# A LayerNorm's transposes: eight row tiles turned by DMA in f16 halves in place of TensorE f32 transposes

## The chip, the cores and the metric

One core of a Trainium2 chip runs the whole program. The time is that of one execution on the device in microseconds; the kernel before was run three times, 1746.54 to 1746.77 us, with a median of 1746.63. A change of time is counted against that median.

## The reference

A transformer block with adaptive LayerNorm over 2048 rows of 512: attention over the last 512 cached keys (32 query heads, 8 key heads), then a GEGLU feed-forward, each behind a LayerNorm whose scale and shift come from a conditioning vector `c`.

```
mod = (silu(c) @ w_mod).reshape(c.shape[0], 6, 1, -1)
sa, ca, ga, sb, cb, gb = (mod[:, 0], ..., mod[:, 5])
h = layernorm(x) * (1 + ca) + sa
x = x + ga * attention(h)          # q = h @ wq, softmax(q k^T / sqrt(128)) v, @ wo
h = layernorm(x) * (1 + cb) + sb   # the second LayerNorm
x = x + gb * ((gelu(h @ w_gate) * (h @ w_up)) @ w_down)
```

All is f32. The kernel keeps f32 exactness on the f16 matrix engine by splitting each operand into two f16 halves, a high one and the remainder, and adding three products of halves.

## The kernel before, in words

The 2048 rows are 16 tiles of 128. Attention runs in two halves of the rows, 0 to 1023 and 1024 to 2047. A loop over steps `t` goes through 512 score tiles (128 queries by 512 keys, one head); 256 belong to the first half of the rows, 256 to the second. In a step TensorE computes one score tile `ps` as three f16 matmuls into one of two PSUM banks, VectorE takes the negated row maximum `nm` (line 974), ScalarE the exponential `ee` (983), two steps later ScalarE scales it into the high f16 half of `p` (995), and three steps later VectorE makes the low half (1000) and SP's queue turns both halves with one DMA transpose, `pt<-p` (1004). Up to three groups of other matmuls follow in each step, popped from a list: the q projection (Strassen products, banks `qa`, `qb`, `qc`), P times V (`po`, which reads `pt` two units of four steps later), and the output projection (`py`). PSUM banks under the tag "acc" are five, handed round in turn; p's f16 tiles are four.

Every engine runs its instructions in the order in which the program gives them while this loop lasts. Work beside the main stream is placed by step: `at(("w", t), fn)` puts `fn`'s instructions behind everything else of step `t`, `("d", t)` behind the low half of p on VectorE. Transfers go through SP's queue in program order; `spare` fills steps that moved nothing with a transfer from a list of due ones.

When the last of the output projections of a row tile is added to `acc` (line 943), `attn_final` is called. For the first eight tiles, which are finished as the second half of the attention begins, it starts the second LayerNorm at once: `ln_tile(2, ti, ...)` returns the steps `stat` (row mean and variance on VectorE, 378 to 382, and the power -0.5 on GpSimd, 388), `norm` (subtract and multiply in place on `acc` on GpSimd, through `pool_ts`, 236), `turn` (four f32 transposes by TensorE into one "acc" bank `pln`, 491), `affine` twice (two ScalarE pieces of 128 columns each from `pln` into `hf` with scale and shift, 499; the second also stores `hf` to DRAM as `hs`), and `parts` twice (f16 high halves on ScalarE, 511, low halves on GpSimd, 513). They are placed 1, 5, 8, 9, 10, 12 and 13 steps after the call. Twelve steps after it the next rows of x are loaded into the tile's `acc` buffer. GpSimd also prepares weights in this time: it scales them (159), makes high halves (155), subtracts for the low halves (156) and forms the Strassen sums (789).

The last eight tiles' second LayerNorm (`ln_turned`, in the feed-forward) is turned by DMA already. The stored `hs` are read again by the `combos` for the feed-forward, from step 478 on. The feed-forward itself follows the loop.

Of the kernel before, what the change touches and what calls it, by code (L numbers as in the profile page):

```python
# [11 lines left out]
F16 = mybir.dt.float16  # L12
BF16 = mybir.dt.bfloat16
AF = mybir.ActivationFunctionType
ALU = mybir.AluOpType
AX = mybir.AxisListType

P = 128
S, D, F = 2048, 512, 1792
HQ, HKV, DH = 32, 8, 128  # L20
W = 512
KT = D // P
# [39 lines left out]
def block_kernel(ctx: ExitStack, tc: tile.TileContext, x, kT, v, wq, wo, wg, wu, wd, cT, wc, wm, out):  # L62
    nc = tc.nc

    const = ctx.enter_context(tc.tile_pool(name="const", bufs=1))
    pool = ctx.enter_context(tc.tile_pool(name="pool", bufs=2))
# [4 lines left out]
    def tmp(name):  # L71
        return pool.tile([P, 512], F32, tag="e", name=name, bufs=NE)

    def raw(name):
        return pool.tile([P, 512], F32, tag="raw", name=name, bufs=NRAW)
# [4 lines left out]
    def bank(tag, name, bufs):  # L80
        return psum.tile([P, 512], F32, tag=tag, name=name, bufs=bufs)
# [9 lines left out]
    def dma(out_, in_):  # L91
        moved[0] += 1
        nc.sync.dma_start(out_, in_)

    def load_acc(i, src, eng=None):
        acc[i] = pool.tile([P, D], F32, tag="acc", name="acc", bufs=2 * QT)
        (eng.dma_start if eng else dma)(acc[i], src)

    def rows_of(t, i):
        return t[i * P:(i + 1) * P, :]  # L100
# [134 lines left out]
    def pool_ts(out, src, a, b=1.0, op0=ALU.mult, op1=ALU.mult):  # L235
        nc.gpsimd.tensor_scalar(out, src, a, b, op0=op0, op1=op1)
# [111 lines left out]
    def spilled(gen, key):  # L348
        if (gen, key) not in hs:
            n = KT if key in (0, 1) else 2  # L350
            hs[gen, key] = dram.tile([P, n, QB], F32, name=f"hs{gen}_{key}")
        return hs[gen, key]

    def block(gen, name):
        if (gen, name) not in BK:
            BK[gen, name] = pool.tile([P, 4, QB], F16, tag="h", name=name, bufs=NB)
        return BK[gen, name]
# [15 lines left out]
    def ln_cols(key):  # L373
        return (1, 0) if key == "a" else (4, 3)

    def ln_stat(a, st, act=False):
        bn = small.tile([P, 6], F32, name="bn")
        nc.vector.bn_stats(bn, a)
        st["mv"] = small.tile([P, 2], F32, name="mv")
        nc.vector.bn_aggr(st["mv"], bn)  # L380
        st["rs"] = small.tile([P, 1], F32, name="rs")
        nc.vector.tensor_scalar(st["rs"], st["mv"][:, 1:2], EPS, None, op0=ALU.add)
        if act:
            st["nm"] = small.tile([P, 1], F32, name="nmean")
            nc.vector.tensor_scalar(st["nm"], st["mv"][:, 0:1], -1.0, None, op0=ALU.mult)

    def ln_power(st):
        nc.gpsimd.tensor_tensor(st["rs"], st["rs"], nhalf, op=ALU.pow)
# [69 lines left out]
    def ln_last(i):  # L458

        st = {}  # L460
        ln_stat(acc[2 * QT + i], st)
        ln_power(st)
        rs, nm = col("kmax", i), col("kinv", i)
        pool_ts(rs, st["rs"], 1.0)
        pool_ts(nm, st["mv"][:, 0:1], st["rs"], -1.0)

    def ln_tile(gen, i, src):
        jsc, jsh = ln_cols("a" if gen < 2 else "f")
        qb, i = divmod(i % (2 * QT), QT)
        st = {}  # L470

        def load():
            if gen == 2:
                st["x"] = src()
            else:
                st["x"] = raw("xs")
                dma(st["x"], src())

        def stat():
            ln_stat(st["x"], st)  # L480
            ln_power(st)

        def norm():
            if gen == 2:
                return pool_ts(st["x"], st["x"], st["mv"][:, 0:1], st["rs"], ALU.subtract, ALU.mult)
            nc.vector.tensor_scalar(st["x"], st["x"], st["mv"][:, 0:1], st["rs"], op0=ALU.subtract, op1=ALU.mult)

        def turn():
            st["ps"] = bank("acc", "pln", NACC)
            for dt in range(KT):  # L490
                nc.tensor.transpose(st["ps"][:, dt * P:(dt + 1) * P], st["x"][:, dt * P:(dt + 1) * P], ident)

        def affine(dts):
            if 0 in dts:
                st["f"] = raw("hf") if gen == 2 else tmp("hf")
            f = st["f"]
            for dt in dts:
                sl = slice(dt * P, (dt + 1) * P)
                nc.scalar.activation(f[:, sl], st["ps"][:, sl], AF.Identity,
                                     scale=cols[:, jsc, dt:dt + 1], bias=cols[:, jsh, dt:dt + 1])  # L500
            if KT - 1 in dts:
                dma(spilled(gen, qb)[:, :, i * P:(i + 1) * P], f.rearrange("p (k q) -> p k q", k=KT))

        def parts(act):
            o = slice(i * P, (i + 1) * P)
            f = st["f"].rearrange("p (k q) -> p k q", k=KT)
            for h, name in enumerate(("b11", "b21") if qb == 0 else (None, "b22")):
                if name:
                    t, src = block(gen, name), f[:, 2 * h:2 * h + 2, :]
                    if act:  # L510
                        nc.scalar.activation(t[:, 0:2, o], src, AF.Copy)
                    else:
                        nc.gpsimd.tensor_tensor(t[:, 2:4, o], src, t[:, 0:2, o], op=ALU.subtract)

        more = [lambda: parts(True), lambda: parts(False)]
        return load, [stat, norm, turn, lambda: affine((0, 1)), lambda: affine((2, 3))] + more

    TURN = {}

# [149 lines left out]
    def k_items(pr):  # L669
        g = pr // 2  # L670
        st, load = reader(kT[g])
        m = {}

        def stat():
            m["m"] = little("lm", 4, dtype=BF16)
            sumsq(m["m"][:, 0:1], st["r"])

        def spread(go=True, ps=None):
            return k_spread(g, m["m"], go, ps)

        def parts(first=False):
            KV[0, pr, 0] = t = get_k()
            if first:
                return split_post(t, st["r"], col("ksc", pr))
            times(st["r"], col("ksc", pr))
            halves(t, st["r"])

        return (load, stat, spread, parts) + ((m,) if pr == 0 else ())
# [33 lines left out]
    def at(key, *fns):  # L722
        later.setdefault(key, []).extend(fns)
# [95 lines left out]
    def plain_steps(key, by):  # L819
        def part(k):  # L820
            SET.setdefault(key, [None, None])[k] = get_w(k)
            if key > 1:
                return soon(split_post(SET[key][k], RAW[key][k], by))
            times(RAW[key][k], by)
            halves(SET[key][k], RAW[key][k])

        return lambda: part(0), lambda: part(1)
# [121 lines left out]
    def attn_final(ti):  # L949
        y1[ti] = dram.tile([P, D], F32, name=f"y{ti}")  # L950
        dma(y1[ti], acc[ti])
        nxt = (ti + 2 * QT) % NT
        if ti < 2 * QT:
            own, steps = ln_tile(2, ti, lambda: acc[ti])
            own()
            for d, fn in zip((1, 5, 8, 9, 10, 12, 13), steps):
                at(("w", now[0] + d), fn)
            at(now[0] + 12, lambda: load_acc(nxt, rows_of(x, nxt)))
        else:
            ln_last(ti - 2 * QT)  # L960
            at(now[0] + 3, lambda: load_acc(nxt, y1[nxt]))
# [31 lines left out]
    def high(t):  # L993
        p16 = pool.tile([P, 2, W], F16, tag="p16", name="p16", bufs=NP16)
        nc.scalar.activation(p16[:, 0, :], E[t]["e"], AF.Copy, scale=E[t]["r"])  # L995
        E[t]["p16"] = p16

    def low(t):
        p16 = E[t]["p16"]
        nc.vector.scalar_tensor_tensor(p16[:, 1, :], E[t]["e"], E[t]["r"], p16[:, 0, :], op0=ALU.mult, op1=ALU.subtract)  # L1000
        u, i = divmod(t, 4)
        if i == 0:
            pT[u] = pool.tile([P, QT, 2 * KT, P], F16, tag="pt", name="pt", bufs=NPT)
        nc.sync.dma_start_transpose(pT[u][:, i], p16.rearrange("p a b -> p (a b)"))
        E.pop(t)
# [196 lines left out]
    for g in range(NG):  # L1202
# [6 lines left out]
        if 0 < g < GW:  # L1209
            a, b = plain_steps(g, by)  # L1210
            sched_pair(g, srcs, t0 - (19 if g > 1 else 13), spread, [(t0 - (13 if g > 1 else 8), a)], [(t0 - (11 if g > 1 else 7), b)])
        elif g >= GW and (not half or pr < GW):
            sched_set(g, srcs, t0, by, spread)
            if not half:
                a, b, c, d, e, f = SETPOS2 if g == GW else SETPOS
# [11 lines left out]
        else:  # L1227
            if g > 0:
                if pr % 2 == 0:
                    load, stat, spread_, parts = k_items(pr)  # L1230
                    sched(t0 - (22 if g > 2 else 20), (load, [stat]))
                    at(("w", t0 - (19 if g > 2 else 17)), spread_)
                load, stat, spread_, parts = k_items(pr)
                sched(t0 - (7 if g > 2 else 8 if g > 1 else 6), (load, [parts if g != 2 else lambda parts=parts: soon(parts(True))]))
                at(t0 - (3 if g > 2 else 1 if g > 1 else 2), lambda pr=pr: store(("k", pr), KV[0, pr, 0]))
                if pr % 2 == 0:
                    load, stat, spread_, parts = v_items(qd)
# [159 lines left out]
    for n in range(NP):  # L1397
        b = T // 2 + 30 + 27 * n
# [167 lines left out]
    for i in range(2 * QT):  # L1566
        q = 7 * (2 + i // 2) + 3 * (i % 2)
        load, norm, split, turn = ln_turned(i)
# [6 lines left out]
    for p in range(2):  # L1575
        q = 51 + 14 * p
# [67 lines left out]
```

## Time and profile before

| | us |
|---|---|
| median of three runs | 1746.63 |
| the profiled execution | 1747.24 |
| its span, first to last instruction | 1745.3 |
| TensorE busy in the span | 1723.9 |
| VectorE busy | 1380.3 |
| ScalarE busy | 1213.7 |
| GpSimd busy | 901.1 |

In the rows of the profile PE is TensorE, PEld its weight loads, DVE VectorE, ACT ScalarE, POOL GpSimd, SPq the instruction queue of SyncE, which issues the DMAs. A timeline row has its start, its duration, engine, line, operation, output and inputs by name, their shapes, and in square brackets how long the engine was idle before it and what ended that. The end of a matmul is modelled and overlaps the next start. Groups that are listed by line give a count and the least, median and largest duration in ns. A line is that of the kernel before; line 87 is the helper that issues all f16 matmuls.

### The profile page before, as it was taken

Reading aid. Unit: us, or ns where it says so; the run is one execution under the profiler, and the core shown is the slowest. Engines: PE = TensorE matmul, PEld = TensorE weight load, DVE = VectorE, ACT = ScalarE, POOL = GpSimd, SP = SyncE. Lnnn points to the kernel's source line nnn. Section 1 sums busy time; section 2 is a strip of 40 time slices with the busy share of each in tenths; the row PEclk is TensorE's granted clock in tenths of the full one; section 3 lists DMA queues with packets and bytes.
Section 4 is the critical chain, followed back from the end, with each engine's and each line's share of the span. In section 5 each row is a group of like instructions: output and inputs, shape, how many; then the busy total and the mean of one; then the engine's idle time right before and its main releaser. Section 6 shows DMA issues by size and latency. Waiting matters only on the chain.

```text
span 1745.3 us, 25819 instructions
## 1 busy us (share of the span) xinstructions
PE 1723.9 (99%) x8080; PEld 793.2 (45%) x8082; DVE 1380.3 (79%) x2404; ACT 1213.7 (70%) x2751; POOL 901.1 (52%) x1120
## 2 busy tenths in 40 slices
PE   7999999999999999999999999999999999999999
PEld 5444444444444444444444444444444444444444
DVE  7898898888889999888888888888886655555555
ACT  6988788888879777888777777877784544323232
POOL 4889778776788884654475565554521224000000
PEclk9999999999999999999999999999999999999999
DMA  7999999999999999999999999999986753252222
GB/s 234 219 206 211 211 215 206 225 209 219 213 219 228 212 205 183 212 208 235 212 201 215 203 220 199 211 214 213 195 184 145 205 174 117 81 183 77 88 75 76
DMA packets 667498, 329.71 MB, mean 189 GB/s; under 512 B 561504, under 2 KB 580192, under 8 KB 667360
## 3 DMA queue, kind: packets, MB, share of 16 engines
q1 hardware_dynamic: 667072, 327.54, 82.0%
q8 instruction: 64, 1.05, 0.3%
q14 instruction: 74, 0.61, 0.1%
q10 hardware_dynamic: 288, 0.52, 0.1%
HBM read 131.73 MB, written 59.90 MB: 110 GB/s over the span
## 4 chain that ended last, share of the span: by engine, by line
PE 87%; DVE 4%; ACT 4%; issue 1%; DMA 1%; POOL 1%; SPq 0%; ACTq 0%; POOLq 0%; DVEq 0%
PE py L87 25%; PE po L87 17%; PE ps L87 16%; PE fa L87 8%; PE qa L87 8%; PE fc L87 4%; PE qc L87 4%; PE qb L87 2%; PE fb L87 2%; ACT ee L983 1%; DVE p L1000 1%; ACT p L995 1%; DVE nm L974 1%; DMA pt<-p 1%; PE pq L87 1%
## 5 line engine op out<-in xcount | busy, mean ns | idle before, releaser
L983 ACT ACTIVATE ee<-ps,nm 128x512 f32<-128x512 f32 x512 | 350.2, 684 | 199.2 <-DVE nm L974 196.5
L1000 DVE SCALAR_TENSOR_TENSOR p<-ee,rr,p 128x512 f16<-128x512 f32 x512 | 460.7, 900 | 5.1 <-ACT p L995 4.7
L974 DVE TENSOR_REDUCE nm<-ps 128x1 f32<-128x512 f32 x512 | 350.3, 684 | 111.5 <-PE ps L87 108.4
L87 PE MATMUL ps<-k,qt 128*128 128x512 f16 x1536 | 414.9, 379 | 5.4 <-ACT ee L983 4.2
L87 PE MATMUL po<-pt,v 128*128 128x512 f16 x1536 | 373.0, 379 | 2.0 <-DMA pt<-p 2.0
L995 ACT ACTIVATE p<-ee,rr 128x512 f16<-128x512 f32 x512 | 364.4, 712 | 13.1 <-DVE rr L991 8.8
L87 PE MATMUL py<-wo,ot 128*128 128x512 f16 x1536 | 371.5, 379 | 0.0
L87 PEld LDWEIGHTS <-w 128*128 128x128 f16 x2184 | 213.5, 98 | 258.1 <-DVE w L1045 0.6
L87 PEld LDWEIGHTS <-v 128*128 128x128 f16 x1536 | 149.9, 98 | 184.3 <-DMA pt<-p 2.5
L87 PEld LDWEIGHTS <-ot 128*128 128x128 f16 x1536 | 150.2, 98 | 181.7 <-DVE ot L731 0.5
L87 PEld LDWEIGHTS <-qt 128*128 128x128 f16 x1536 | 145.9, 98 | 176.7 <-issue 4.3
L87 PE MATMUL py<-wo,at 128*128 128x512 f16 x672 | 160.5, 379 | 0.0
L943 DVE SCALAR_TENSOR_TENSOR acc<-py,dysc,acc 128x512 f32<-128x512 f32 x112 | 81.5, 747 | 51.1 <-PE py L87 51.1
L731 DVE SCALAR_TENSOR_TENSOR ot<-po,ot 128x512 f16<-128x512 f32 x128 | 87.7, 685 | 33.0 <-ACT ot L730 32.2
L87 PEld LDWEIGHTS <-at 128*128 128x128 f16 x672 | 65.7, 98 | 79.3
L983 ACT ACTIVATION_READ_ACCUMULATOR ee<-ps,nm 128x1 f32 x512 | 99.9, 195 | 0.0
L943 DVE SCALAR_TENSOR_TENSOR acc<-py,ysc,acc 128x512 f32<-128x512 f32 x128 | 94.7, 740 | 6.2 <-PE py L87 6.2
L1281 ACT ACTIVATE at<-fg 128x512 f16<-128x512 f32 x56 | 35.2, 628 | 72.2 <-DVE fg L1279 71.9
L87 PE MATMUL qa<-t,w 128*128 128x512 f16 x348 | 84.9, 379 | 0.0
L87 PE MATMUL fa<-t,w 128*128 128x512 f16 x336 | 82.0, 379 | 0.0
L730 ACT ACTIVATE ot<-po 128x512 f16<-128x512 f32 x128 | 73.9, 577 | 5.0 <-PE po L87 5.0
L232 POOL TENSOR_TENSOR lw<-lw,half__86 128x1 f32<-128x1 f32 x37 | 22.1, 598 | 104.6 <-DVE lw L182 104.5
(222 smaller groups left out, 2379.9 us busy)
## 6 DMA issues: line engine op xcount, KB each, us to landing
w<-kept SPq DMA_DIRECT2D x123, 256.0 KB, 3.2
wo<-kept SPq DMA_DIRECT2D x60, 256.0 KB, 3.8
raw<-in_wo SPq DMA_DIRECT2D x56, 256.0 KB, 3.3
kept<-stage SPq DMA_DIRECT2D x56, 256.0 KB, 3.4
kept<-w SPq DMA_DIRECT2D x39, 256.0 KB, 3.4
rw<-in_wq SPq DMA_DIRECT2D x38, 256.0 KB, 3.2
hs<-hf SPq DMA_DIRECT2D x32, 256.0 KB, 2.9
pt<-p SPq DMA_TRANSPOSE x512, 3.5
```

The lines of the kernel that those rows point to most:

```text
L87: nc.tensor.matmul(ps, a, b, start=first and n == 0, stop=last and n == 2, skip_group_check=chain)
L232: nc.gpsimd.tensor_tensor(out, out, half_, op=ALU.pow)
L730: nc.scalar.activation(t[:, 0, :], src, AF.Copy, scale=scale)
L731: return lambda: nc.vector.scalar_tensor_tensor(t[:, 1, :], src, scale, t[:, 0, :], op0=ALU.mult, op1=ALU.subtract)
L943: nc.vector.scalar_tensor_tensor(acc[ti], st["p"], by, acc[ti], op0=ALU.mult, op1=ALU.add)
L974: nc.vector.tensor_reduce(nm, E[t]["ps"], axis=AX.X, op=ALU.max, negate=True)
L983: nc.scalar.activation(e, E[t]["ps"], AF.Exp, bias=E[t]["nm"], scale=1.0, accum_out=sm[:, t % 2:t % 2 + 1])
L995: nc.scalar.activation(p16[:, 0, :], E[t]["e"], AF.Copy, scale=E[t]["r"])
L1000: nc.vector.scalar_tensor_tensor(p16[:, 1, :], E[t]["e"], E[t]["r"], p16[:, 0, :], op0=ALU.mult, op1=ALU.subtract)
L1281: nc.scalar.activation(t[:, 0, :], g, AF.Copy)
```

## The change

In `ln_tile` with `gen == 2` the step `turn` becomes four steps. `high` copies the normed rows to f16 on ScalarE; `low` subtracts that from them on GpSimd; `turn_dma` turns both halves with one DMA transpose on SP's queue into `lnt`; `joined` adds the two turned halves on VectorE into the f32 tile `hf`. `affine` then works in place on `hf` in SBUF instead of reading a PSUM bank. The steps stand 1, 4, 5, 6, 7, 10, 10, 11, 12 and 13 steps after the call. The new tiles `lnh` and `lnt` have two buffers each; the scratch memory for GpSimd's own DMA descriptors is set to 1024.

```diff
+        def high():
+            st["h"] = pool.tile([P, 2, D], F16, tag="lnh", name="lnh", bufs=2)
+            nc.scalar.activation(st["h"][:, 0, :], st["x"], AF.Copy)
+
+        def low():
+            nc.gpsimd.tensor_tensor(st["h"][:, 1, :], st["x"], st["h"][:, 0, :], op=ALU.subtract)
+
+        def turn_dma():
+            st["t"] = pool.tile([P, 2, KT, P], F16, tag="lnt", name="lnt", bufs=2)
+            nc.sync.dma_start_transpose(st["t"].rearrange("p h k q -> p (h k) q"), st["h"].rearrange("p a b -> p (a b)"))
+
+        def joined():
+            st["f"] = raw("hf")
+            f = st["f"].rearrange("p (k q) -> p k q", k=KT)
+            nc.vector.tensor_tensor(f, st["t"][:, 0], st["t"][:, 1], op=ALU.add)
+            st["ps"] = st["f"]
+
         def affine(dts):
-            if 0 in dts:
-                st["f"] = raw("hf") if gen == 2 else tmp("hf")
+            if 0 in dts and gen < 2:
+                st["f"] = tmp("hf")
...
-        return load, [stat, norm, turn, lambda: affine((0, 1)), lambda: affine((2, 3))] + more
+        turns = [high, low, turn_dma, joined] if gen == 2 else [turn]
+        return load, [stat, norm] + turns + [lambda: affine((0, 1)), lambda: affine((2, 3))] + more
...
-            for d, fn in zip((1, 5, 8, 9, 10, 12, 13), steps):
+            for d, fn in zip((1, 4, 5, 6, 7, 10, 10, 11, 12, 13), steps):
...
-    nc = _bacc.Bacc("TRN2", target_bir_lowering=False, num_devices=1)
+    nc = _bacc.Bacc("TRN2", target_bir_lowering=False, num_devices=1, dynamic_dma_scratch_size=1024)
```

## The prediction

> **What bounds the kernel now.** First the page's busy shares, then the busy time by stretch for the two places around the change, then TensorE's own timeline there.
>
> ```profile
> span 1745.3 us, 25819 instructions
> PE 1723.9 (99%) x8080; PEld 793.2 (45%) x8082; DVE 1380.3 (79%) x2404; ACT 1213.7 (70%) x2751; POOL 901.1 (52%) x1120
> ```
>
> ```profile
> 690.00:800.00 110.00, 108.87 (x524) 51.38 (x522) 95.23 (x179) 93.23 (x229) 59.60 (x62) 1.00 0.96 207
> 800.00:840.00 40.00, 40.00 (x189) 18.17 (x188) 33.04 (x59) 32.59 (x77) 24.65 (x34) 1.00 1.07 233
> ...
> 720.00:735.00 15.00, 14.37 (x72) 6.90 (x70) 14.70 (x29) 11.54 (x28) 14.42 (x14) 1.00 1.07 218
> ```
>
> The columns of a stretch are its length, then busy time and count of TensorE, its weight loads, VectorE, ScalarE and GpSimd, then the granted clock, the DMA engines' share and GB/s. TensorE is busy for 99% of the span at a granted clock of 1.00, so time that is taken from its stream or put into it stays to the end. The eight tiles of the change lie between 690 and 800 us. VectorE works 95.23 of those 110 us, ScalarE 93.23, GpSimd 59.60: none is full on the whole, but between 720 and 735 VectorE has 0.30 us left and GpSimd 0.58. Whatever the change adds there pushes back what stands behind it.
>
> **What is removed.** 32 f32 transposes, four per tile (I number the tiles 0 to 7).
>
> ```profile
> 699.56 0.60 PE L491 MATMUL pln<-ident,acc 128*128 128x128 f32 x4
> 700.00 0.81 PE L87 MATMUL ps<-k,qt 128*128 128x512 f16 x3
> 700.64 2.11 PE L87 MATMUL po<-pt,v 128*128 128x512 f16 x9
> ...
> 730.01 0.81 PE L87 MATMUL po<-pt,v 128*128 128x512 f16 x3
> 731.45 0.63 PE L491 MATMUL pln<-ident,acc 128*128 128x128 f32 x4 [0.63 <-POOL w L155]
> 731.91 0.81 PE L87 MATMUL ps<-k,qt 128*128 128x512 f16 x3
> ...
> 773.18 0.81 PE L87 MATMUL po<-pt,v 128*128 128x512 f16 x3
> 774.31 0.63 PE L491 MATMUL pln<-ident,acc 128*128 128x128 f32 x4 [0.32 <-ACT hf L499]
> 774.77 0.81 PE L87 MATMUL ps<-k,qt 128*128 128x512 f16 x3
> ```
>
> Durations of matmuls overlap, so I count from start to start. Three matmuls of 512 columns take 700.64 - 700.00 = 0.64 us. Tile 0 costs 700.00 - 699.56 = 0.44. Tiles 1, 2, 4, 5 and 6 show the same 0.43 to 0.44 and no wait; with tile 0 that is 2.6. Tile 3 also waits: 731.91 - (730.01 + 0.64) = 1.26. Tile 7: 774.77 - (773.18 + 0.64) = 0.95. Sum 4.8 us.
>
> ```profile
> 730.85 0.46 ACT L499 ACTIVATE hf<-pln,cols 128x128 f32<-128x128 f32 x1
> ```
>
> I put the wait at 731.45 down to this row: it ends at 731.31 and is the last to read tile 2's PSUM bank, and the five "acc" banks are handed round, so tile 3's transposes get that one; GpSimd's norm, the other thing that they need, was long done. Without transposes these eight banks are not asked for, and both waits go. If they only move to the next user of a bank, 4.8 becomes 2.6 + 0.46 + 0.46 = 3.5.
>
> **What is added, per tile.** A ScalarE copy to f16, a GpSimd subtraction, one DMA transpose of 128x1024 on SP's queue, a VectorE addition. The affine steps read SBUF in place of PSUM. The rows, by source line, are counts and least, median and largest ns: a ScalarE copy and a VectorE sum of the same size first,
>
> ```profile
> L1281 ACT ACTIVATE at<-fg x56: 612/630/632, 1335.8 to 1734.5; 128x512 f16<-128x512 f32 x56
> L440 DVE TENSOR_TENSOR b<-hf,b x3: 676/676/677, 20.6 to 40.4; 128x512 f16<-128x512 f32 x3
> ```
>
> then GpSimd's subtraction in two stretches, and the transposes of p from 720 to 750.
>
> ```profile
> L156 POOL TENSOR_TENSOR w<-rw,w x3: 1157/1157/1161, 603.0 to 618.0; 128x512 f16<-128x512 f32 x3
> L156 POOL TENSOR_TENSOR w<-rw,w x2: 1600/1632/1663, 731.5 to 737.4; 128x512 f16<-128x512 f32 x2
> ```
>
> ```profile
> L1004 SPq DMA_TRANSPOSE pt<-p x11: 1231/1232/1348, 721.7 to 749.5; - x11
> DMA to landing us min/median/max: 3.0/3.5/4.9
> ```
>
> ScalarE: 8 x 0.63 = 5.0 us of the 16.8 it has free. VectorE: 8 x 0.68 = 5.4 of 14.8 free; the row has the operation and the size with two SBUF inputs, only the types differ, and I allow 0.5 to 1.2 each. GpSimd: 1.16 to 1.66 each, 9.3 to 13.3 of 50 free; I take 1.16, the middle of the first stretch, since the block of GpSimd's work below already holds stretched rows. The affine from SBUF: the pair of L511 at 736.33, quoted below, reads twice the width from SBUF in 0.71, L499's pair at 716.82 takes 0.83, so I take no change, and 0.2 a pair either way. SP: 1.23 of issue and 3.5 to landing, like the eleven of p in these 30 us. The DMA engines carry it: eight more of 256 KB over 110 us raise 207 GB/s by 19 to 226, and the stretch from 800 to 840 ran 233 GB/s with TensorE busy 40.00 of 40. By busy time alone all of this is hidden and 4.8 stands. The store of a tile's turned rows comes one step later and trades places on SP with a few fetches; the same transfers go out, and the stored rows are read only from step 478 on. The smaller pool that is set aside for GpSimd's own DMA descriptors costs nothing, as no data transfer here is issued by GpSimd; its bound is the 1.94 us that lie around the span, either way.
>
> **What is moved, and the new wait.** The order of the new program puts the norm on GpSimd four steps behind the row sum instead of five, and ScalarE's copy one step behind that norm, where formerly TensorE came three steps behind it. A step is one score tile, half of 739.68 - 734.50 below, 2.59 us. Engines run in order, so a late norm now stops ScalarE, and with it the exponentials.
>
> GpSimd's, ScalarE's and TensorE's timelines:
>
> ```profile
> 716.70 0.69 POOL L159 TENSOR_SCALAR rw<-rw,wsc 128x512 f32<-128x512 f32 x1
> 718.73 1.16 POOL L156 TENSOR_TENSOR w<-rw,w 128x512 f16<-128x512 f32 x1
> ...
> 733.12 2.51 POOL L236 TENSOR_SCALAR acc<-acc,mv,rs 128x512 f32<-128x512 f32 x1
> 745.02 1.30 POOL L513 TENSOR_TENSOR b<-hf,b 128x256 f16<-128x256 f32 x2 [4.35 <-ACT b L511]
> ```
>
> ```profile
> 716.21 0.74 ACT L995 ACTIVATE p<-ee,rr 128x512 f16<-128x512 f32 x1
> 716.82 0.83 ACT L499 ACTIVATE hf<-pln,cols 128x128 f32<-128x128 f32 x2
> 725.03 0.58 ACT L730 ACTIVATE ot<-po 128x512 f16<-128x512 f32 x1
> 736.33 0.71 ACT L511 ACTIVATE b<-hf 128x256 f16<-128x256 f32 x2
> 737.63 0.69 ACT L983 ACTIVATE ee<-ps,nm 128x512 f32<-128x512 f32 x1
> ```
>
> ```profile
> 734.50 0.81 PE L87 MATMUL ps<-k,qt 128*128 128x512 f16 x3
> 739.68 0.81 PE L87 MATMUL ps<-k,qt 128*128 128x512 f16 x3
> ```
>
> GpSimd works without a gap from 716.70 to the end of tile 4's norm, 733.12 + 2.51 = 735.63: 18.93 us. In the new order tile 2's subtraction stands ahead of this block and tile 3's inside it. The first waits for ScalarE's copy of tile 2, which comes after the row at 716.21, two affine pieces and itself: 716.21 + 0.74 + 0.83 + 0.63 = 718.4, less the 0.87 that tiles 0 and 1 have given, 717.5. Then 1.16 + 18.93 + 1.16 puts the end of tile 4's norm at 738.8. ScalarE gets to tile 4's copy where the pair at 736.33 ends, 737.04; I move that up by 1.0, not by the 2.6 that TensorE would have gained from tiles 0 to 3, because VectorE, which feeds it, is full there. So ScalarE stands for about 2.8 us, then copies until 739.4, and its next exponential ends at 740.1 instead of 738.32. That one must free the score bank for the second score group after it, old start 739.68, new 739.68 - 2.6 = 737.1. TensorE waits 3.0 us. Bounds: with subtractions of 1.66 it is 4.0; if ScalarE's copy of tile 2 or GpSimd's block runs 3 us shorter than I think, nothing.
>
> At tile 3 the norm follows the row at 718.73, whose end is 3.19 us into the block: 717.5 + 1.16 + 3.19 + 2.51 = 724.4; ScalarE comes there after the row at 725.03, at 725.61 - 0.87 = 724.7, so no wait, with 0.3 in hand. At tile 5 GpSimd has the 4.35 us that it sat idle before 745.02, more than the 3.2 by which it is late at tile 4. SP also stands: in the new order tile 3's transpose comes ahead of the transpose of p at 732.14, and its subtraction ends only some 4.5 us before tile 4's norm (a split of L155 and L156 and the norm lie between), near 734.
>
> ```profile
> 732.14 1.29 SPq L1004 DMA_TRANSPOSE pt<-p  x1
> ```
>
> ```profile
> 741.62 0.81 PE L87 MATMUL po<-pt,v 128*128 128x512 f16 x3
> ```
>
> It then goes out near 736 and with 3.5 lands at 739.5. It feeds the group at 741.62, which would come at 741.62 - 2.6 = 739.0, so this wait is covered by the 3.0 at tile 4 and costs at most 0.5 on its own. VectorE's addition for tile 3 stands for its landing at about 737.5, before VectorE gets there.
>
> Sum: -4.8 + 3.0 = -1.8 us on the span of 1745.3, 1743.5. The profiled execution took 1747.24, 0.61 above the median of the runs, 1746.63; from the median I get 1744.8.
>
> **The rivals.** (A) All cover holds and the whole 4.8 stays: 1741.8, up to 1743.1 if little is lost. For it: GpSimd has 50 us free over the stretch and only one of eight tiles is clearly late. Against it: the 14.42 of 15.
>
> (B) Slower than before: the norm is late not at one tile but at 3, 4 and 5, and ScalarE stands behind GpSimd at each. The price is tile 4's, 3 x 3.0 = 9.0: 1746.6 - 4.8 + 9.0 = 1750.8. It decides as soon as GpSimd is half a microsecond later than reckoned at tile 3, where 0.3 is in hand, and takes up the 4.35 idle us before tile 5 as well. Against it: a wait at one tile holds up TensorE and gives GpSimd time for the next.
>
> (C) VectorE becomes the bound between 719 and 740.
>
> ```profile
> 723.39 1.22 DVE L1000 SCALAR_TENSOR_TENSOR p<-ee,rr,p 128x512 f16<-128x512 f32 x1
> 726.88 0.73 DVE L1000 SCALAR_TENSOR_TENSOR p<-ee,rr,p 128x512 f16<-128x512 f32 x1
> ```
>
> The same operation takes 1.22 beside GpSimd's subtractions and 0.73 without. With no room there, TensorE cannot use what tiles 2 and 3 give, 0.43 + 1.26 = 1.7, and the rest goes as forecast: 1744.8 + 1.7 = 1746.5. Against it: the exponential at 737.63 ends 739.68 - 738.32 = 1.36 us before its bank is wanted. The Trainium skill, "SBUF — State Buffer", section "Who interferes with whom", says more: a VectorE instruction with two SBUF inputs and a GpSimd instruction that reads SBUF exclude each other, and the loser waits for all of the other. By that rule, the two rows agree in kind, with 0.49 us. An estimate by that page, if every addition met a whole norm like the 2.51 at 733.12, is 8 x (0.68 + 2.51) = 25.5 us against 14.8 free, 10.7 too many, about 1752.5; the rows show a fifth of that wait.
>
> **How the numbers follow.** Forecast 0.47, A 0.28, B 0.12, C 0.13. About 0.2%, 3.5 us, is what a measurement of this kernel can tell from no change: below 1743.1 lies A, 0.28; above 1750.1 lies B, 0.12; the forecast and C, 0.60, lie within. The range takes in A's end, 1741.8, and goes to 1748.3, past C and the forecast with subtractions of 1.66 and a copy or two more that wait; B is left out. The forecast's own range is 1743.2 to 1746.
>
> **What would show it.** The eight groups of transposes are gone, and between 690 and 725 TensorE runs through. Right: one wait of score matmuls for an exponential near 738 to 741, ScalarE idle before tile 4's copy with GpSimd as releaser, 2 to 4 us, the other copies near none. Wrong towards A: no such wait, TensorE busy 110.00 of 110. Wrong towards B: ScalarE's copies wait at three tiles or more, and po waits for transposes of p on SP. Wrong towards C: additions above 1 us, and score matmuls that wait with ScalarE waiting for VectorE's maxima. An addition that waits long for its transpose would contradict the 3.5 us of landing.

## The result, and the profile after

| | before | after |
|---|---|---|
| median of four runs each | 1746.70 | 1755.09 |
| lowest to highest | 1746.54 to 1749.31 | 1754.26 to 1755.90 |
| span of the profiled execution | 1745.3 | 1752.5 |

The ratio is 1.0044, with a 95% interval from 1.0027 to 1.0062: the change makes the kernel 8.4 us slower. The forecast, 1744.8 with a range to 1748.3, was wrong, and on the wrong side.

First the page's shares and the busy time by stretch, in the columns explained above:

```profile
span 1752.5 us, 25788 instructions
PE 1723.0 (98%) x8048; PEld 789.7 (45%) x8050; DVE 1384.8 (79%) x2412; ACT 1217.5 (69%) x2759; POOL 909.7 (52%) x1128
```

```profile
690.00:800.00 110.00, 99.42 (x450) 44.12 (x448) 95.67 (x175) 91.88 (x220) 69.17 (x69) 0.98 0.99 212
720.00:735.00 15.00, 14.36 (x66) 6.24 (x64) 14.86 (x28) 11.67 (x29) 14.51 (x15) 1.00 1.10 231
800.00:840.00 40.00, 40.00 (x189) 18.13 (x187) 33.90 (x60) 32.66 (x79) 20.88 (x28) 1.00 1.06 233
```

The 32 transposes are gone, yet TensorE stands 10.6 of the 110 us, where it stood 1.1 before. From 800 on it is full again. So the loss lies wholly in the stretch of the eight tiles. TensorE's timeline names the waits:

```profile
724.34 0.81 PE L87 MATMUL ps<-k,qt 128*128 128x512 f16 x3 [0.62 <-ACT ee L1001]
735.68 0.81 PE L87 MATMUL ps<-k,qt 128*128 128x512 f16 x3 [0.64 <-ACT ee L1001]
739.80 0.81 PE L87 MATMUL ps<-k,qt 128*128 128x512 f16 x3 [1.37 <-ACT ee L1001]
754.24 0.81 PE L87 MATMUL ps<-k,qt 128*128 128x512 f16 x3 [1.31 <-ACT ee L1001]
...
774.49 0.81 PE L87 MATMUL ps<-k,qt 128*128 128x512 f16 x3 [1.17 <-ACT ee L1001]
791.92 1.14 PE L87 MATMUL ps<-k,qt 128*128 128x512 f16 x3 [4.32 <-ACT ee L1001]
```

The waits for a PSUM bank are gone as forecast. In their place seven score groups wait for an exponential instead of the one that I expected; with a `qa` group at 760.53 (0.31) the short waits come to 6.3 us. The long one, 4.32 us, stands where I expected nothing. Its cause is on VectorE:

```profile
783.62 0.97 DVE L1018 SCALAR_TENSOR_TENSOR p<-ee,rr,p 128x512 f16<-128x512 f32 x1
789.60 0.69 DVE L507 TENSOR_TENSOR hf<-lnt 128x512 f32<-128x512 f16 x1 [5.01 <-POOL b L530]
790.21 0.68 DVE L992 TENSOR_REDUCE nm<-ps 128x1 f32<-128x512 f32 x1
```

```profile
787.79 1.15 POOL L156 TENSOR_TENSOR stage<-rw,stage 128x512 f16<-128x512 f32 x1
788.90 0.67 POOL L530 TENSOR_TENSOR b<-hf,b 128x256 f16<-128x256 f32 x1
```

The first rows are VectorE's, the second GpSimd's. Tile 7's addition does not wait for the rows it reads. It waits until GpSimd has read tile 6's `hf` (line 530): `joined` takes its output from the five "raw" buffers that are handed round, and the one that is due is still tile 6's. GpSimd reaches that read late, behind two splits of staged weights. The kernel before takes `hf` from the same five buffers, one step earlier, and has no such wait. Behind the addition on VectorE stands the next row maximum, so ScalarE and TensorE stand too.

The stretch after this wait costs once more:

```profile
786.00:792.00 6.00, 1.69 (x9) 0.69 (x8) 2.40 (x4) 1.64 (x5) 3.48 (x4) 1.00 0.46 131
792.00:796.00 4.00, 4.00 (x12) 1.41 (x12) 3.42 (x7) 3.90 (x9) 0.00 (x0) 0.57 0.99 129
```

TensorE comes back at a granted clock of 0.57, and 4.00 x 0.43 = 1.7 us are lost. In the sum of this trace, -4.8 + 6.3 + 4.3 + 1.7 = 7.5 against 7.2 in the span.

### The profile page after: what moved, and what is told of

The parts are those of the page before. It is cut to its first block, busy times and chain, and to the rows that moved or that the text cites. A ratio compares the mean times of both kernels' runs of the same rounds, so it can differ in the third digit from the quotient of the medians.

```text
span 1752.5 us, 25788 instructions
## 1 busy us (share of the span) xinstructions
PE 1723.0 (98%) x8048; PEld 789.7 (45%) x8050; DVE 1384.8 (79%) x2412; ACT 1217.5 (69%) x2759; POOL 909.7 (52%) x1128
## 3 DMA queue, kind: packets, MB, share of 16 engines
q8 instruction: 63, 1.03, 0.3%
## 4 chain that ended last, share of the span: by engine, by line
PE 87%; DVE 5%; ACT 4%; POOL 2%; issue 1%; DMA 1%; SPq 0%; POOLq 0%; ACTq 0%; DVEq 0%
PE py L87 25%; PE po L87 16%; PE ps L87 16%; PE fa L87 8%; PE qa L87 8%; PE fc L87 4%; PE qc L87 4%; PE fb L87 2%; PE qb L87 2%; DVE p L1018 1%; ACT ee L1001 1%; DVE nm L992 1%; ACT p L1013 1%; PE pq L87 1%; DVE qt L749 1%
```

## The experiments

Each difference is that of the medians against the kernel before on the same chip (1747.68, 1747.59, 1746.80 and 1747.15 in the four groups of runs). One ratio's interval is about 0.09% either way, 1.6 us (copy_later and affine_9, with five runs, about 0.13%; the changed kernel itself, with four, 0.18% or 3.1 us), so sizes under that are read with care. A profile shows one execution: it names places, the medians give sizes.

| kernel | difference, us | ratio, 95% interval |
|---|---|---|
| own_hf | +4.0 | 1.0023 [1.0014, 1.0033] |
| no_add | +1.35 | 1.0006 [0.9996, 1.0015] |
| copy_later | +6.1 | 1.0035 [1.0022, 1.0048] |
| early_bank | -1.3 | 0.9991 [0.9982, 1.0001] |
| pool_halves | +3.1 | 1.0019 [1.0010, 1.0027] |
| no_turn | +4.9 | 1.0026 [1.0016, 1.0037] |
| pool_no_add | -1.5 | 0.9993 [0.9985, 1.0002] |
| early_bank_5 | -1.2 | 0.9994 [0.9985, 1.0003] |
| bare | -1.4 | 0.9994 [0.9985, 1.0003] |
| bare_late | +2.4 | 1.0010 [1.0002, 1.0019] |
| copies_late | +4.4 | 1.0024 [1.0015, 1.0033] |
| affine_9 | +6.4 | 1.0036 [1.0023, 1.0048] |
| bare_rw | -3.2 | 0.9981 [0.9973, 0.9990] |
| before_rw | -0.2 | 0.9998 [0.9989, 1.0007] |
| early_rw | -1.8 | 0.9988 [0.9979, 0.9996] |
| own_rw | +2.35 | 1.0013 [1.0004, 1.0022] |

### The reused buffer: own_hf

```diff
-            st["f"] = raw("hf")
+            st["f"] = pool.tile([P, D], F32, tag="hfj", name="hf", bufs=2)
```

> The joined rows get two buffers of their own instead of one of the five that the weight loads and stages share. Theory R (reused buffer): in the changed kernel the sum of tile 7 is written into the buffer that held tile 6, and VectorE stands 5.0 us until GpSimd has read tile 6's low halves from it; TensorE stands 4.32 and then runs some 4 us at a granted clock near 0.57, 1.7 more. All 6.0 goes: 1755.1 - 6.0 = 1749.1, no wait over 1 us in front of the sum of tile 7, and some 6 us of short score waits stay. Rival G (GpSimd late in general, whatever the buffer): the wait moves to the next thing that needs GpSimd, 1753 or more.

The median falls by 4.4 us, from +8.4 to +4.0, and not by the 6.0 of theory R. VectorE's 5.01 us is gone, and so are TensorE's 4.32 and the low clock. The short waits stand as they were. Two others come up in TensorE's timeline:

```profile
798.57 2.10 PE L87 MATMUL po<-pt,v 128*128 128x512 f16 x9 [1.47 <-DMA pt<-p]
...
803.93 0.82 PE L87 MATMUL ps<-k,qt 128*128 128x512 f16 x3 [0.66 <-DMA k<-kept]
```

They are 2.1 us, and 6.0 - 2.1 = 3.9 is near the 4.4. So the buffer is a cause, and about half of the loss; the other half has others. The edit also leaves the five buffers to their other users; no run separates what that is worth.

### The additions on VectorE: no_add

no_add is own_hf with

```diff
-            nc.vector.tensor_tensor(f, st["t"][:, 0], st["t"][:, 1], op=ALU.add)
-            st["ps"] = st["f"]
+            st["ps"] = st["t"][:, 0].rearrange("p k q -> p (k q)")
```

> As own_hf, but VectorE's addition is left out and the scale and shift read the turned high halves alone, so the low halves do not enter the result. Theory V (VectorE's eight additions, 5.4 us and more, push the row maxima back where VectorE is full): at least half of the 6.3 us of short score waits of the changed kernel goes, 3 us or more below own_hf, 1746 or less. Theory G (ScalarE's copies stand behind GpSimd's norms): at most 1 us below own_hf, the waits of 1.4 and 1.2 us near tiles 4 and 7 stay.

Beside own_hf the median falls by 2.6 us. Of the waits behind exponentials 0.62 and 0.64 become one of 0.44 and 1.31 becomes 0.60; 1.37 and 1.16 stay. The waits for `pt` and `k` shrink to 0.34 and 0.38. The additions, which I had costed at nothing, are a part; the edit also takes away ScalarE's waits for them (2.9 us in own_hf), and the 2.6 us is the price of both. Not all of it is GpSimd's doing, for only two of the eight are much stretched in the changed kernel (1.15 at 729.52, 1.10 at 739.31), and a third in own_hf (1.21 at 785.38):

```profile
L507 DVE TENSOR_TENSOR hf<-lnt x8: 679/688/1146, 705.1 to 789.6; 128x512 f32<-128x512 f16 x8
```

This row groups the changed kernel's additions: least, median and largest ns.

### ScalarE behind GpSimd's norm: copy_later and pool_halves

ScalarE's copies met a late norm at two tiles in the changed kernel. Its timeline at tile 4, and GpSimd's norm there:

```profile
734.85 0.69 ACT L1001 ACTIVATE ee<-ps,nm 128x512 f32<-128x512 f32 x1 [0.75 <-DVE nm L992]
...
736.86 0.71 ACT L528 ACTIVATE b<-hf 128x256 f16<-128x256 f32 x2
738.45 0.63 ACT L495 ACTIVATE lnh<-acc 128x512 f16<-128x512 f32 x1 [0.88 <-POOL acc L236]
738.99 0.67 ACT L1001 ACTIVATE ee<-ps,nm 128x512 f32<-128x512 f32 x1
```

```profile
735.91 2.51 POOL L236 TENSOR_SCALAR acc<-acc,mv,rs 128x512 f32<-128x512 f32 x1
```

copy_later is own_hf with

```diff
-            for d, fn in zip((1, 4, 5, 6, 7, 10, 10, 11, 12, 13), steps):
+            for d, fn in zip((1, 4, 7, 8, 9, 12, 12, 13, 14, 15), steps):
```

> As own_hf, with ScalarE's copy and everything behind it two steps later, so that three steps lie between norm and copy instead of one. Theory G: the waits of ScalarE's copies for the norm (0.88 at tile 4, 1.29 at tile 7) go, and with them the score waits of 1.37 and 1.17 us: 2.5 us below own_hf, about 1746.6. Theory V: the same number of additions on VectorE, the same time as own_hf within 0.7 us.

The copies no longer stand, but the time rises 2.1 us above own_hf. TensorE now waits 2.16 us at 727.10 and 1.55 at 773.86, and ScalarE's affines stand 6.8 us for additions (2.9 in own_hf). The granted clock falls behind the first of them:

```profile
727.00:731.00 4.00, 3.90 (x13) 1.54 (x13) 3.46 (x8) 3.97 (x12) 3.84 (x6) 0.67 0.65 162
731.00:735.00 4.00, 4.00 (x18) 1.72 (x17) 3.35 (x7) 3.97 (x11) 3.84 (x6) 0.90 1.24 154
```

That is 4.00 x 0.33 + 4.00 x 0.10 = 1.7 us more. Moving the steps moved the waits: theory G's 2.5 us less and theory V's "the same time" both failed.

pool_halves is own_hf with

```diff
-            nc.scalar.activation(st["h"][:, 0, :], st["x"], AF.Copy)
+            nc.gpsimd.tensor_scalar(st["h"][:, 0, :], st["x"], 1.0, 1.0, op0=ALU.mult, op1=ALU.mult)
```

> The changed kernel with the joined rows in buffers of their own (own_hf), and the high half written by GpSimd instead of ScalarE. GpSimd gets 8 copies of about 0.81 us (its halves of the stages at line 155 take that), ScalarE loses 8 of 0.62 and its two stands behind the norm (0.88 and 1.29 us). Theory G (ScalarE, by the copies and their stands, delays the exponentials): the waits of 1.36 and 1.17 us of the score matmuls go, and with the 5 us of copies part of the others too: own_hf less 2.5 to 5 us, 0.1 to 2.5 us on either side of the kernel before (ratio about 0.9993 to 1.0009). Theory V (VectorE's additions and their waits make all of it): within 0.7 us of own_hf, ratio 1.0019 to 1.0027. A third way, GpSimd late: the low halves come 0.8 us and more later, and an addition at the head of VectorE's queue waits for its rows longer than before: own_hf plus 1 us, ratio 1.003, with VectorE idle before an addition.

0.9 us under own_hf, short of G's 2.5 to 5 and just past V's 0.7; a difference of this size is within the intervals and decides neither. The third way is there as well:

```profile
728.66 0.68 DVE L772 TENSOR_TENSOR qd<-u,qc 128x512 f32<-128x512 f32 x1
731.30 1.14 DVE L507 TENSOR_TENSOR hf<-lnt 128x512 f32<-128x512 f16 x1 [1.95 <-DMA lnt<-lnh]
```

With both halves on GpSimd tile 3's rows land later, and VectorE stands 1.95 us with the addition at the head of its queue. TensorE waits 1.77 us at 734.06.

### Both together: pool_no_add

It carries no_add's edit and pool_halves' edit.

> no_add (no addition of the halves, the low halves don't enter the output) with the high half written by GpSimd too. If the additions on VectorE and the copies on ScalarE with their stands (V and G together) are the whole loss, what is left is the gain of the removed transposes less the waits that neither makes (0.3 + 0.3 us for pt and k): before less 3.5 to 4.8 us, about 1743 to 1744 us, ratio 0.9973 to 0.9980. If the copies have no part in it, it equals no_add: ratio 1.0008. If it lies between, the rest of the waits has a third cause (the low halves on GpSimd or the DMA).

It lies between, at -1.5: taking the copies off ScalarE is worth 2.8 us beside no_add, the additions 4.6 beside pool_halves but 2.6 beside own_hf. The two costs are not independent. With neither of them 3.3 of the 4.8 us that the transposes took are still missing, so a third cause was open.

### The DMA transposes: no_turn

own_hf, with the addition reading `st["h"]` in place of a turned tile:

```diff
-            st["t"] = pool.tile([P, 2, KT, P], F16, tag="lnt", name="lnt", bufs=2)
-            nc.sync.dma_start_transpose(st["t"].rearrange("p h k q -> p (h k) q"), st["h"].rearrange("p a b -> p (a b)"))
+            st["t"] = st["h"].rearrange("p h (k q) -> p h k q", k=KT)
```

> own_hf without its 8 DMA transposes: the addition reads the two halves as GpSimd and ScalarE left them, so that the rows aren't turned. Theory S (the transposes on SP hold up the p transposes and the loads behind them): the waits of 1.47 us for pt and 0.66 us for k near 800 go: own_hf less 2.1 us, about 1749.5 us or a ratio of 1.0011. Against S: those two waits come from the rest of SP's queue, the span stays within 0.5 us of own_hf, ratio 1.0020 to 1.0026; the waits behind the exponentials (6.25 us in sum) stay in both.

No gain: +4.9, its interval overlaps own_hf's. The wait for `pt` stays, 1.46 us against 1.47:

```profile
798.59 2.10 PE L87 MATMUL po<-pt,v 128*128 128x512 f16 x9 [1.46 <-DMA pt<-p]
```

Only the 0.66 for `k` is gone. The DMA transposes themselves, their issue on SP and their traffic cost nothing that shows, as forecast.

### The removal by itself: bare, bare_late, copies_late

bare is the kernel before with one edit; the affines read the rows as they lie:

```diff
         def turn():
+            if gen == 2:
+                st["ps"] = st["x"]
+                return
             st["ps"] = bank("acc", "pln", NACC)
```

> The kernel before without TensorE's transposes of the second LayerNorm: the affines read the rows as they lie, so that the rows aren't turned; nothing is added. If the first term of the sum holds (the removal is worth 4.8 us when nothing takes its place): 4.8 us under the kernel before, ratio 0.9973, span about 1740.5 us. If ScalarE and VectorE have no slack there (theory L: TensorE only comes sooner to score matmuls that wait for an exponential): the gain is cut to 1 to 3 us, ratio 0.9983 to 0.9994, with new waits of the score matmuls that add up to the rest.

This fells the first term of the sum. Without the transposes and with nothing in their place the kernel gains 1.4 us and not 4.8. TensorE's timeline has the rest:

```profile
738.26 0.81 PE L87 MATMUL ps<-k,qt 128*128 128x512 f16 x3 [0.56 <-ACT ee L986]
751.85 0.81 PE L87 MATMUL ps<-k,qt 128*128 128x512 f16 x3 [0.24 <-ACT ee L986]
767.85 0.81 PE L87 MATMUL ps<-k,qt 128*128 128x512 f16 x3 [0.72 <-ACT ee L986]
794.54 3.60 PE L87 MATMUL po<-pt,v 128*128 128x512 f16 x9 [2.58 <-DMA pt<-p]
```

Three times TensorE runs into an exponential that does not come as much sooner as TensorE does, 1.5 us (the one before 738.26 ends at 738.12, in the kernel before at 738.32). Then it waits 2.58 us for a transposed p. The profiled run is the slowest of bare's 11 (span 1746.8; the median of their spans is 1743.6); the low clock follows this wait too (last section).

bare_late has the norm and the affines where the changed kernel has them:

```diff
-            for d, fn in zip((1, 5, 8, 9, 10, 12, 13), steps):
+            for d, fn in zip((1, 4, 5, 10, 11, 12, 13), steps):
```

> The same with the norm at step 4 and the affines at steps 10 and 11, where the changed kernel has them (before: 5, 9 and 10). Theory P (the place of the affines, close ahead of the copies at step 12, makes part of the short waits): 1 to 3 us over bare, with score matmuls waiting for exponentials. Against P: within 0.5 us of bare.

3.8 us over bare, but not in the way that theory P has it. The view of ScalarE's waits gives one stand:

```profile
ACT hf L502 <- POOL b L516: 5.5, 1, 5.5
```

It is the reused buffer again, this time before tile 7's first affine: a step later in the program the buffer due for this `hf` is one that GpSimd has still to read, and TensorE stands 3.78 us behind it. So the place of the affines matters through the ring of buffers.

copies_late adds ScalarE's copy to bare_late (nobody reads it):

```diff
             if gen == 2:
+                st["h"] = pool.tile([P, 2, D], F16, tag="lnh", name="lnh", bufs=2)
+                nc.scalar.activation(st["h"][:, 0, :], st["x"], AF.Copy)
                 st["ps"] = st["x"]
```

> bare_late with ScalarE's 16-bit copy of the normed rows at step 5 as in the changed kernel (nobody reads it), no GpSimd halves, no DMA, no addition. Theory G (ScalarE by the copies and their stands behind the norm): 2.5 us or more over bare_late, with the waits of 1.36 and 1.17 us near 740 and 775, ScalarE idle before two copies. If ScalarE has room for the copies: within 0.7 us of bare_late.

2.0 us over bare_late, less than the 2.5 expected. (This kernel also has the smaller scratch memory of the changed one.) One copy stands 1.3 us behind the norm; the wait of 1.17 near 772 is there, the one near 740 is 0.28. The stand at the reused buffer is in both kernels:

```profile
ACT hf L504 <- POOL b L518: 5.6, 1, 5.6
```

So the difference is that of the copies: TensorE's waits of up to 1.2 us add up to 2.85 here and to 1.03 in bare_late. Most of the copies' price is there without additions. In the profiled executions the clock fell behind the long wait in bare_late alone (last section), which may hide a part of it.

### An earlier step: affine_9

own_hf with

```diff
-            for d, fn in zip((1, 4, 5, 6, 7, 10, 10, 11, 12, 13), steps):
+            for d, fn in zip((1, 4, 5, 6, 7, 9, 9, 10, 12, 13), steps):
```

> own_hf with the addition and the affines one step earlier (9, 9 and 10, the affines where the kernel before has them). Theory P: own_hf less 1 to 2.5 us, ratio 1.0009 to 1.0017. Against P, or where the rows land too late for step 9 (3.5 us after the issue at step 7, two steps of some 3.3 us each): own_hf or above it, ratio 1.0023 to 1.004, with VectorE waiting for the landing at an addition.

2.4 us above own_hf. VectorE stands at additions:

```profile
DVE hf L507 <- DMA lnt<-lnh: 2.6, 3, 1.2
```

Theory P falls here too: of the steps tried for the addition, 9, 10 and 12 (copy_later), none is free. At 9 some rows have not landed yet.

### What stands behind the wait for pt: bare_rw, before_rw, own_rw

bare's SP queue ahead of its wait at 794.54:

```profile
785.84 1.27 SPq L1007 DMA_TRANSPOSE pt<-p  x1
789.52 0.35 SPq L93 DMA_DIRECT2D rw<-in_wu  x1
789.94 0.53 SPq L93 DMA_DIRECT2D kept<-stage  x1
790.58 1.31 SPq L1007 DMA_TRANSPOSE pt<-p  x1
```

The queue issues nothing from 787.11 to 789.52. The load at 789.52 needs an "rw" buffer that GpSimd reads until 789.50, and GpSimd is late because its own split stood 4.19 us for the store of an earlier stage:

```profile
787.33 0.62 POOL L155 TENSOR_SCALAR stage<-rw 128x512 f16<-128x512 f32 x1 [4.19 <-DMA kept<-stage]
788.03 1.47 POOL L156 TENSOR_TENSOR stage<-rw,stage 128x512 f16<-128x512 f32 x1
```

The transposes of p stand in the queue behind this load. It comes no sooner when TensorE does; in the kernel before it goes out at

```profile
789.27 0.35 SPq L93 DMA_DIRECT2D rw<-in_wu  x1
```

The test is one buffer more:

```diff
-                t = pool.tile([P, 512], F32, tag="rw", name="rw", bufs=NRW)
+                t = pool.tile([P, 512], F32, tag="rw", name="rw", bufs=NRW + 1)
```

with, in bare_rw, before_rw and early_rw, the smaller scratch memory of the changed kernel to make room.

> bare (no transposes, the rows aren't turned) with a third buffer for the loads at line 776 (tag rw), the order written out unchanged. In bare TensorE stands 2.58 us for pt near 794, because SP's queue stands at a load until GpSimd has read the rw buffer, and the p transposes lie behind it. Theory Q (that stand of SP's queue caps the gain): the wait near 794 goes, and 2 us or more of the 4.8 come back: ratio 0.9975 to 0.9983 against the kernel before, 1742.5 to 1744 us. Against Q: the wait stays at over 1.5 us, as p itself is late, and the ratio stays at 0.9992 to 0.9996.

> The kernel before with the third rw buffer alone: the control for bare_rw. TensorE's wait for pt there is 0.18 us, so that 0.2 us at most can be gained: ratio 0.9998 to 1.0002 by Q. If the buffer helps or hurts by itself (loads earlier, other meetings of the queues), it shows here, and bare_rw is read against this one.

> own_hf (the changed kernel, joined rows in buffers of their own) with the third rw buffer. By Q its waits for pt (1.47 us) and k (0.66 us) near 800 go: 1.5 to 2.1 us under own_hf, ratio 1.0011 to 1.0014. If its p's are late by ScalarE instead, the ratio stays at 1.0020 to 1.0026.

All three times come out by theory Q. bare_rw: -3.2, and no wait for pt; the load now goes out ahead of the transpose, without a pause:

```profile
784.71 1.04 SPq L93 DMA_DIRECT2D rw<-in_wu  x1
785.80 0.53 SPq L93 DMA_DIRECT2D kept<-stage  x1
786.44 1.35 SPq L1007 DMA_TRANSPOSE pt<-p  x1
```

What is still missing of 4.8, 1.6 us, is the three waits for exponentials (0.56, 0.25 and 0.73 in bare_rw). before_rw gains 0.2: the kernel before had no use for the buffer, which also clears the scratch setting. own_rw lies 1.6 us under own_hf; its wait for `pt` is gone as expected, that for `k` is not: 0.47.

### A version that beats both: early_bank, early_rw

early_bank leaves LayerNorm's work on the engines where the kernel before has it. It puts the affines one step earlier, so that the bank is read out before the next tile's transposes ask for it:

```diff
-            for d, fn in zip((1, 5, 8, 9, 10, 12, 13), steps):
+            for d, fn in zip((1, 5, 8, 8, 9, 12, 13), steps):
```

> The kernel before, with the two affine pairs one step earlier (8 and 9 steps after the call instead of 9 and 10), so that the bank of the f32 transposes is read out sooner. If tile 3's and tile 7's transposes wait for the bank of the tile before (0.8 and 0.5 us over the pitch), both go: 1746.7 - 1.3 = 1745.4. If they wait for something else, or the earlier pairs delay ScalarE, no change, 1746.7.

> The kernel before with its affines one step earlier, timed again for a tight interval: 1.3 us under the kernel before by the two waits for a bank that go (0.63 and 0.32 us, and what hung on them), ratio 0.9993 with an interval that ends below 1. If the first timing (ratio 0.9991) was chance, 1.0000.

Twice 1.2 to 1.3 us, as expected, and both waits for a bank are gone; but both intervals reach just past 1, also the second, which I expected to end below it. With the third rw buffer:

> early_bank (the affines one step earlier) with the third rw buffer. By Q its wait for pt near 793 (0.57 and 0.70 us in two profiles) goes, on top of the 1.2 us of early_bank: ratio 0.9988 to 0.9992, interval below 1. If not, it equals early_bank, 0.9994.

-1.8 us, the interval is below 1, and TensorE has no gap left in the stretch, with all its transposes in place:

```profile
690.00:800.00 110.00, 110.00 (x531) 52.33 (x530) 96.77 (x182) 95.51 (x232) 60.22 (x64) 1.00 1.00 221
```

## Why the prediction was wrong

**The removal, -4.8 us: wrong, the first step that failed.** I took a busy TensorE, "so time that is taken from its stream or put into it stays to the end". bare shows 1.4. The exponentials take back 1.5, and a p transpose, held in SP's queue by a load, another 1.8 (bare_rw has them again). In the kernel before these two limits lay just behind TensorE. For the exponential before 739.68 the prediction has the distance, 1.36 us under rival C, less than the 2.6 that TensorE was to gain by then; the sum does not use it. The wait for `pt` stands in that trace and I did not quote it:

```profile
793.90 2.10 PE L87 MATMUL po<-pt,v 128*128 128x512 f16 x9 [0.18 <-DMA pt<-p]
```

The 4.8 was the work and the waits removed; what can be gained is at most the distance to whatever is ready next. The waits for a bank did go, and did not move to another user; early_bank bears out that they were waits for a bank.

**"By busy time alone all of this is hidden": wrong.** The additions cost 2.6 us (no_add beside own_hf), the copies 2.0 to 2.8 (copies_late beside bare_late, pool_no_add beside no_add). A share of free time over 110 us says nothing for a short instruction that stands in order between a row maximum and an exponential. The DMA transposes at nothing: right (no_turn). The affines from SBUF at no change: right within the 0.2 allowed (0.88 us the pair at 715.82 in the changed kernel, 0.83 at 716.82 before). I found no cost of the low halves on GpSimd by themselves: pool_no_add, which has them, is as fast as bare.

**The output buffer: not asked for.** The prediction priced the addition's duration and inputs, and wrote of a tile that "VectorE's addition for tile 3 stands for its landing". That it writes into a ring of five, whose former user GpSimd may still read, has no term in the sum. It is the largest single one, 4.4 us by own_hf, the clock included. bare_late shows that later steps alone can bring it about: with `hf` taken at step 9 (bare) the same ring costs no wait, with the norm at step 4 and `hf` at step 10 a stand of 5.5 us.

**The wait at tile 4, 3.0 us: right in kind, too large.** GpSimd ended tile 4's norm at 735.91 + 2.51 = 738.42, forecast 738.8. ScalarE stood 0.88 and not 2.8: it was ready for the copy at 738.45 - 0.88 = 737.57, and not at 736.0 as forecast, in part because VectorE held it up before (its exponential at 734.85 waited 0.75 for a row maximum). TensorE stood 1.37. A second stand, at tile 7 (1.29 on ScalarE, 1.17 on TensorE), has no term in the sum.

**The rivals.** None has the time. A is excluded. B (1750.8) asked for copies that stand at three tiles or more; there were two. C came true in part: two additions above 1 us and VectorE busy 14.86 of 15 between 720 and 735. The rule of the Trainium skill that I cited there ("SBUF — State Buffer", section "Who interferes with whom"), that a VectorE instruction with two SBUF inputs and a GpSimd reader exclude each other, agrees in kind with 1.15 against 0.68 us, in two additions of eight; beside the other six GpSimd was idle, near the end of an instruction or at a power of one column. The largest estimate by it, some 1752.5, lies nearest to the result, yet by a mechanism that these rows show only twice.

**The ledger by medians.** bare -1.4, the copies +2.8, the additions +2.6, the buffer +4.4: 8.4 against 8.4 measured. The last three are differences along one chain of kernels, from pool_no_add over no_add and own_hf to the changed one, so that their sum has to fit; what the ledger tests is only that the chain's start, pool_no_add (-1.5), equals bare (-1.4). Each step carries some 1.6 us of uncertainty, the buffer's 3, and the costs depend on their order (the additions are 2.6 or 4.6).

## What to carry to other kernels

Before crediting a bound engine with removed work, look in the trace for the next thing that it would wait for, above all in waits of a few tenths: the gain is at most the distance to that, and running the kernel with the work left out measures it. Cost a new instruction by its place in its engine's order and by all that it waits for: its inputs, the engine ahead, and who last reads the buffer it writes. Small waits at the bound engine itself (two of 0.63 and 0.32) were worth more here, by moving one step and adding one buffer, than moving a whole stage to idle engines.

## What was not expected of the hardware

After two to four microseconds without matmuls TensorE came back at a granted clock of about half, but not always. The changed kernel had 0.57 over 4 us after an idle time of 4.32. copy_later's wait of 2.16 (its windows stand above) and bare's of 2.58 did the same, bare_late's of 3.78 too, and copies_late's of 3.73 did not; the windows are, in this order, bare, bare_late and copies_late:

```profile
794.00:798.00 4.00, 3.46 (x10) 1.25 (x10) 1.45 (x3) 1.51 (x4) 0.00 (x0) 0.57 1.03 265
```

```profile
786.00:791.00 5.00, 4.78 (x12) 1.70 (x12) 3.21 (x6) 4.87 (x13) 0.19 (x1) 0.50 0.78 182
```

```profile
790.00:794.00 4.00, 3.90 (x19) 1.66 (x17) 3.23 (x6) 3.90 (x10) 0.21 (x1) 1.00 0.56 154
```

The 1.83 us of pool_no_add left the clock at 1.00. The Trainium skill, "TensorE: Matmul & The Clock Gate", section "Part 1: The HAM clock gate (the "warmup" mystery)", says that the clock falls to half after an idle window of about 3.4 us and that this window runs freely. The half clock agrees. The length does not: 2.16 us were enough in copy_later. That 3.73 us weren't in copies_late would fit a window that runs freely, but no run here shows the window. So a wait of 2 us and more at TensorE cost 1.7 to 2.5 us on top in four of these five traces (4.00 x 0.43 in two, 4.00 x 0.33 + 4.00 x 0.10 in copy_later, 5.00 x 0.50 in bare_late), and nothing in copies_late.
